# Exp of the routing logits comes third in its list, and early rows' turns and one piece move ahead of the last waits

## The chip, the cores and the metric

The kernel runs on one core of one Trainium2 chip. The metric is the device time of one execution in microseconds (us). The times shown are those of whole executions; the profile is of one further execution, with its own time.

## What is computed

Attention over short windows feeds a mixture of experts with one expert for each token. The arithmetic that matters here, cut from the reference:

```python
# attention: q, k, v are (4, 8, 768, 64); 8 memory rows are in front of each window
for c in range(S // 32):                       # chunks of 32 queries
    k_full = concat(mem_k, k[32*c - 16 : 32*c + 40])
    a = softmax(q_c @ k_full.T / 8)            # sum + 1e-9
    out[c] = a @ v_full
x = out.transpose(0, 2, 1, 3).reshape(3072, 512)
# mixture of experts: 8 experts, 512 -> 1024 -> 512
logits = x @ w_gate
expert_idx = argmax(logits)
probs = exp(logits - max); probs /= probs.sum() + 1e-9
y = relu(x @ w1[expert_idx]) @ w2[expert_idx]
return probs[expert_idx] * y
```

## The kernel before

**Attention.** The 3,072 tokens are 32 blocks of 96 queries. One loop runs over the blocks; its order was written out by hand (`tc.manual_schedule()`), so each engine does its work in the order in which the code issues it. In step `i`, TensorE (PE) makes the scores of block `i`, turns (transposes) the queries of block `i + 2` (`turn_q`), multiplies the first four heads of block `i - 1` by the values (`values(i - 1, 0)`), turns the result `x` of block `i - 2` (`turn_xb`), makes the gate logits of block `i - 3`, does the other four heads (`values(i - 1, 1)`), and turns the keys of block `i + 4` (`turn_k`). ScalarE (ACT) makes the exponentials of the scores (L676, tile `ex`), copies turned queries out of PSUM (L627, `qT`) and turned `x` (L699, `xT`). VectorE (DVE) divides by the softmax sums (L690 and L692, into `xr`), copies turned keys (L645, `kT`) and logits (L1065, `lg`).

**Routing.** The blocks form seven groups (6, 6, 5, 5, 4, 3, 3 blocks). When a group's last logits are there, `routed(g)` puts a list of small steps into `work`: kind "v" for DVE, "p" for PE, "s" for a scatter. `routing(n, kinds)` takes up to `n` steps from the front while their kind is in `kinds`. The loop calls it three times in each step: for a "p" before the values, for 3 "v" steps (5 after step 23) between `values(i - 1, 0)` and `turn_xb`, and for 5 (6 after step 23) at the end, behind `turn_k`. The "v" steps are `top` (L727), `eq` (L731), `weigh` (L734), `first` (L738), `one` (L741, which also issues GpSimd's (POOL) running counts `seen`, L743) and `less` (L746, a subtraction on DVE followed by the Exp of the logits on ACT, L747); then come `total`, `guard`, `inverse` and the labels (L767 to L779). The "p" step `rank` multiplies `onehot` and `seen` on PE; `own`, `row` and `where` (L756 to L763) make row numbers of it. `hold_back` moves "s" steps from the front of `work` to `spread`, and `scatter_some(1)` issues one of these on POOL's queue: an indirect DMA that writes a block's rows of `xr` to `x_dram` (L801), issued only behind PE's latest instruction in program order.

**Early rows.** After 22 blocks, up to 256 rows of expert 0 are gathered from `x_dram` by two indirect DMAs (L880, tile `xe0`). When they are there, PE works on them to fill its waits: `early_ops` holds two turns (`turn_early`, tile `tx`, copied by ACT at L993 into `x0T`), eight pieces of the first layer (`first(f)`, tile `ph`, eight matmuls of 128x256 each, ended by ACT's Relu at L1005), and eight of the second layer (tile `py`, L1014). `do_early(n)` issues the next `n`.

**The tail.** After the loop, the last blocks are finished by hand-ordered lines (from `room_for_x()` on): values and logits of the last blocks, routing of the last two groups, counts of all experts (`count_up`), five gathers of expert 0's rows (`fetch_x(0)`), with early pieces in between. Then eight experts run one after the other, each as products on PE that are planned beforehand. The turned tiles of the attention phase (`tqk`, `tx`) share two PSUM buffers (`ps_t`) in rotation; logits, values and ranks share two banks (`ps_o`); early pieces use the two buffers of the scores (`ps_s`).

Between these lines stand SyncE's (SP) loads: queries, keys and values for the blocks, weights of expert 0 from step 24 on (two pieces of 512 KB in a step), and two loads of 2 MB for expert 1 at the start of the tail.

Of the kernel before, what the change touches and what calls it, by code (L numbers as in the profile page):

```python
# [504 lines left out]
def ordinary(ctx, tc, q, k, v, mem_k, mem_v, moe_w_gate, moe_w1, moe_w2, out, good):  # L505
# [187 lines left out]
    def turn_xb(i):  # L693
        s = st[i]
        tx = ps_t.tile([128, DM // 128, QB], F32, tag="t", name="tx")
        for c in range(DM // 128):
            turn(tx[:, c], s["x"][:, 128 * c : 128 * c + 128], ident[0:QB, 0:QB])
        s["xT"] = apool.tile([128, DM // 128, QB], F32, name="xT")
        nc.scalar.copy(s["xT"], tx)  # L699
# [18 lines left out]
    def routed(g):  # L718

        t0, t1 = GROUPS[g]  # L720
        n, sl = t1 - t0, slice(t0, t1)
        revs = bc(rev[0:QB], 1, n)
        s = {}

        def top():
            s["top"] = small([QB, n], "ltop")
            nc.vector.reduce_max(s["top"], lgs[g], axis=AX_X)  # L727

        def eq():
            s["eq"] = small([QB, n, E], "eq")  # L730
            nc.vector.tensor_tensor(s["eq"], lgs[g], bc(s["top"], 2, E), op=OP.is_equal)  # L731

        def weigh():
            nc.vector.tensor_tensor(s["eq"], s["eq"], revs, op=OP.mult)  # L734

        def first():
            s["first"] = small([QB, n], "first")
            nc.vector.reduce_max(s["first"], s["eq"], axis=AX_X)  # L738

        def one():  # L740
            nc.vector.tensor_tensor(onehot[:, sl], revs, bc(s["first"], 2, E), op=OP.is_equal)  # L741
            for t in range(t0, t1):
                nc.gpsimd.tensor_tensor(seen[:, t + 1], seen[:, t], onehot[:, t], op=OP.add)  # L743

        def less():
            nc.vector.tensor_tensor(lgs[g], lgs[g], bc(s["top"], 2, E), op=OP.subtract)  # L746
            nc.scalar.activation(lgs[g], lgs[g], AF.Exp)  # L747

        def rank():
            rk = s["rk"] = cur["bank"][0:QB, 4 * (D + 1) : 4 * (D + 1) + n * E].rearrange("p (t e) -> p t e", e=E)  # L750
            mm(rk, lhsT=tri[0:QB, 0:QB], rhs=onehot[:, sl], start=True, stop=False)
            mm(rk, lhsT=ones[0:QB, 0:QB], rhs=seen[:, sl], start=False, stop=True)

        def own():
            s["own"] = small([QB, n, E], "own")
            nc.vector.tensor_tensor(s["own"], s["rk"], onehot[:, sl], op=OP.mult)  # L756

        def row():
            s["row"] = small([QB, n], "row")
            nc.vector.reduce_sum(s["row"], s["own"], axis=AX_X)  # L760

        def where():
            nc.vector.tensor_copy(dest[:, sl], s["row"])  # L763

        def total():
            s["total"] = small([QB, n], "total")
            nc.vector.reduce_sum(s["total"], lgs[g], axis=AX_X)  # L767

        def guard():
            nc.vector.tensor_scalar(s["total"], s["total"], 1e-9, None, op0=OP.add)  # L770

        def inverse():
            s["inv"] = small([QB, n], "tinv")
            nc.vector.reciprocal(s["inv"], s["total"])

        def labels(a, e):
            def put():
                nc.vector.tensor_copy(xr[:, a % NXR : a % NXR + e - a, DM + 1], s["inv"][:, a - t0 : e - t0])
                nc.gpsimd.tensor_copy(xr[:, a % NXR : a % NXR + e - a, DM].bitcast(I32), token[0:QB, a:e])  # L779

            return put

        puts = []
        for a in range(t0, t1):
            if a == t0 or a % NXR == 0:
                puts.append(("v", labels(a, min(t1, (a // NXR + 1) * NXR))))
        v = [("v", f) for f in (top, eq, weigh, first, one, less)]
        u = [("v", f) for f in (total, guard, inverse)] + puts
        w = [("p", rank)] + [("v", f) for f in (own, row, where)]
        return v + u + w + [("s", lambda t=t: scatter_one(t)) for t in range(t0, t1)]  # L790
# [38 lines left out]
    def routing(n, kinds="v"):  # L829
        while work and n and work[0][0] in kinds:  # L830
            kind, f = work.pop(0)
            f()
            n -= kind != "s"

    def hold_back():

        while work and work[0][0] == "s":
            spread.append(work.pop(0)[1])

    def scatter_some(n):  # L840
        while spread and n:
            spread.pop(0)()
            n -= 1
# [180 lines left out]
    def do_early(n):  # L1024
        for _ in range(min(n, len(early_ops))):
            early_ops.pop(0)()

    with tc.manual_schedule():
        load_k(0)
        load_q(0)  # L1030
        load_v(0)
        load_k(1)
        load_v(1)
        load_q(1)
        load_k(2)
        load_v(2)
        load_q(2)
        turn_k(0)
        turn_k(1)
        turn_q(0)  # L1040
        turn_q(1)
        for i in range(NB):
            if i % 2 == 0 and i // 2 + 3 < NSB:
                load_q(i // 2 + 3)
            if i % 2 == 1 and (i + 7) // 2 - 1 < NSB and (i + 7) // 2 - 1 >= 3:
                load_k((i + 7) // 2 - 1)
            need(i + 3, load_v)
            scores(i)
            scatter_some(1)
            if i == 0:  # L1050
                turn_k(2)
                turn_k(3)
            need(i + 2, turn_q)
            banks = [ps_o.tile([128, 512], F32, tag="o", name="o") for _ in range(2)]
            cur["bank"] = banks[0]
            routing(1, "p")
            if i >= 1:
                values(i - 1, 0, banks[0])
            routing(5 if i > 23 else 3)
            need(i - 2, turn_xb)  # L1060
            late = logits(i - 3, banks[1]) if i >= 3 else None
            if i >= 1:
                values(i - 1, 1, banks[1])
            if late:
                nc.vector.tensor_copy(*late)  # L1065
            scatter_some(1)
            need(i + 4, turn_k)
            routing(6 if i > 23 else 5)
            hold_back()
            for g in range(len(GROUPS)):  # L1070
                if i - 3 == GROUPS[g][1] - 1:
                    work.extend(routed(g))
            if i == 24:
                fetch_w(0, 4)
            if i >= 24:
                fetch_piece(1)
                fetch_piece(1)
            if len(scatters) >= EARLY and "early" not in cur:
                cur["early"] = i
                early_count(banks[0])  # L1080
                early_gather()

        early_rows()
        n = NB

        def bank_pair():
            banks = [ps_o.tile([128, 512], F32, tag="o", name="o") for _ in range(2)]
            cur["bank"] = banks[0]
            return banks

        room_for_x()
        banks = bank_pair()
        values(n - 1, 0, banks[0])
        routing(1, "p")
        scatter_some(1)
        turn_xb(n - 2)
        late = logits(n - 3, banks[1])
        values(n - 1, 1, banks[1])  # L1100
        scatter_some(1)
        nc.vector.tensor_copy(*late)
        routing(99, "v")
        fetch_w(1, 1)
        fetch_piece(99)
        turn_xb(n - 1)
        banks = bank_pair()
        late = logits(n - 2, banks[1])
        nc.vector.tensor_copy(*late)
        hold_back()  # L1110
        do_early(2)
        scatter_some(1)
        routing(1, "p")
        routing(99, "v")
        hold_back()
        banks = bank_pair()
        late = logits(n - 1, banks[1])
        nc.vector.tensor_copy(*late)
        work.extend(routed(len(GROUPS) - 1))
        routing(99)  # L1120
        check_sums()
        do_early(2)
        scatter_some(1)
        routing(1, "p")
        routing(99, "v")
        hold_back()
        do_early(1)
        scatter_some(1)
        count_up()
        fetch_x(0)  # L1130
        first_sums()
        while spread:
            do_early(1)
            scatter_some(1)
        index = [nc.tensor.value_load(cases[0:1, e : e + 1], min_val=0, max_val=len(ARMS) - 1) for e in range(E)]
        rv = nc.values_load(good[0:1, 0:1], min_val=0, max_val=1)
        tc.switch_hint({mybir.EngineType.PE: index[0]}, len(ARMS), "expert0")
        nc.tensor.addr_align(PAGE, 0, 0)
        do_early(len(early_ops))
# [470 lines left out]
```

## Time and profile before

| | |
|---|---|
| Time of the kernel before, 3 runs | median 545.87 us (544.91 to 546.52) |
| Profiled execution, its own time | 544.41 us |
| Its span, first to last instruction | 542.4 us |
| Outside the span | 2.0 us |
| PE busy | 509.0 us, 94% of the span |
| DVE, ACT, POOL busy | 301.1, 244.7 and 155.5 us (56%, 45%, 29%) |
| Attention loop, from the first scores | 12.5 to about 157 us |
| Tail up to expert 0's first turn | about 157 to 200.4 us |
| Experts | 200.4 us to the end |
| Mean granted clock of TensorE | 0.988 |

Times in the profile count from the first instruction. "PEld" is the load of a matmul's stationary operand, which overlaps PE. In a timeline, a line reads: start, length, engine, line of the kernel, operation, tile written, tiles read, shapes, count; a bracket gives the idle time of the engine before it and what ended it. "L511" and "L516" are the two helpers through which all matmuls and turns go, so PE's lines are told apart by their tiles.

### The profile page before, as it was taken

The page shows a single profiled execution, that of the slowest core. Times are in us where ns is not written, and L with a number is a line of the kernel's source. Part 1 is how long each engine was busy: PE and PEld are TensorE (multiplying, and loading weights), DVE is VectorE, ACT ScalarE, POOL GpSimd, SP SyncE. Part 2 cuts the span into 40 slices and gives each one's busy share as a digit, 9 for nine tenths or more (in the row PEclk, how much of TensorE's full clock was granted, in tenths as well). Part 3 has the DMA queues.
Part 4 walks back from the last instruction along what each step waited for, and adds up shares of the span by engine and source line. Part 5 has one row for each costly group of instructions (what it writes and reads, how often), then busy time and mean ns, then how long its engine had stood idle before and what let it go on. Part 6 is the DMA issues. An engine that isn't in the chain of part 4 may idle for free.

```text
span 542.4 us, 9575 instructions
## 1 busy us (share of the span) xinstructions
PE 509.0 (94%) x3666; PEld 475.4 (88%) x3666; DVE 301.1 (56%) x567; ACT 244.7 (45%) x443; POOL 155.5 (29%) x186
## 2 busy tenths in 40 slices
PE   3889999999989989999999999999999999999991
PEld 2789999999988649999999999987779999999980
DVE  3445666566544517868846457543634777853610
ACT  2446565655632126466553264244215637454311
POOL 2000031313354513526134134212322434412002
PEclk9999999999997999999999999999999999999997
DMA  9999998999992310554615154340415344300002
GB/s 158 173 176 177 156 210 173 206 177 294 283 364 102 95 26 39 188 180 171 219 38 190 39 187 167 109 177 30 181 27 195 118 132 186 79 15 12 1 1 82
DMA packets 81348, 75.01 MB, mean 138 GB/s; under 512 B 39542, under 2 KB 64374, under 8 KB 81280
## 3 DMA queue, kind: packets, MB, share of 16 engines
q1 hardware_dynamic: 71840, 54.60, 41.0%
q0 software_dynamic: 8768, 19.29, 10.8%
q8 instruction: 46, 0.75, 0.6%
q10 hardware_dynamic: 672, 0.18, 0.1%
q14 instruction: 22, 0.18, 0.1%
HBM read 66.13 MB, written 17.50 MB: 154 GB/s over the span
## 4 chain that ended last, share of the span: by engine, by line
PE 81%; issue 9%; DMA 4%; POOL 2%; ACT 1%; DVE 1%; SPq 1%; POOLq 0%; another core or an unknown queue 0%
PE sum_p L511 20%; PE sum_r L511 13%; PE sum_q L511 13%; PE o L511 11%; PE sc L511 7%; PE tqk L516 4%; PE sum_x L516 3%; PE ph L511 3%; DMA kn<-in_k_dram 3%; PE py L511 3%; PE sum_q L516 2%; PE tx L516 2%; POOL out_dram L1275 2%; DMA cst<-c_pack 1%; ACT qT L627 1%
## 5 line engine op out<-in xcount | busy, mean ns | idle before, releaser
L1275 POOL DMA_INDIRECT out_dram<-y,xe x42 | 50.9, 1211 | 181.6 <-PE sum_q L511 62.6
L1292 POOL DMA_INDIRECT xe<-x_dram,rows x35 | 50.6, 1446 | 49.9 <-PE sum_r L511 29.3
L676 ACT ACTIVATE ex<-sc,cst 128x256 f32<-128x256 f32 x96 | 38.4, 470 | 49.9 <-PE sc L511 48.5
L1226 ACT COPY sum_r<-sum_p 128x640 f32<-128x640 f32 x48 | 32.5, 677 | 47.4 <-PE sum_p L511 45.6
L511 PE MATMUL o<-v,ex 128*96 128x65 f32 x512 | 53.9, 249 | 0.0
L511 PE MATMUL sc<-qT,kT 128*128 128x192 f32 x256 | 49.3, 337 | 1.5 <-ACT qT L627 1.5
L511 PEld LDWEIGHTS o<-v,ex 128*96 128x96 f32 x512 | 48.5, 165 | 0.0
L511 PE MATMUL sum_p<-xsT,w 128*128 128x136 f32 (+6 forms) x256 | 47.6, 329 | 0.5
L801 POOL DMA_INDIRECT x_dram<-xr,dest x32 | 30.1, 942 | 59.0 <-PE tqk L516 29.8
L511 PE MATMUL sum_r<-t,w 128*128 128x136 f32 (+6 forms) x256 | 45.8, 326 | 0.0
L511 PE MATMUL sum_p<-t,s 128*128 128x136 f32 (+6 forms) x256 | 45.6, 326 | 0.0
L511 PE MATMUL sum_q<-t,s 128*128 128x136 f32 (+6 forms) x256 | 45.1, 324 | 0.0
L645 DVE COPY kT<-tqk 64x384 f32<-64x384 f32 x64 | 35.5, 554 | 15.6 <-PE tqk L516 14.9
L511 PEld LDWEIGHTS sum_p<-xsT,w 128*128 128x128 f32 x256 | 39.7, 190 | 4.8 <-issue 2.1
L511 PE MATMUL sum_p<-h,w 128*128 128x136 f32 (+6 forms) x256 | 43.8, 324 | 0.0
L511 PEld LDWEIGHTS sc<-qT,kT 128*128 128x128 f32 x256 | 42.0, 195 | 1.9 <-issue 1.4
L511 PEld LDWEIGHTS sum_p<-t,s 128*128 128x128 f32 x256 | 39.7, 190 | 2.6
L511 PEld LDWEIGHTS sum_r<-t,w 128*128 128x128 f32 x256 | 39.6, 190 | 2.6
L511 PEld LDWEIGHTS sum_q<-t,s 128*128 128x128 f32 x256 | 39.8, 190 | 2.3
L511 PEld LDWEIGHTS sum_p<-h,w 128*128 128x128 f32 x256 | 39.5, 190 | 2.3
L1223 DVE TENSOR_TENSOR h<-sum_p,kept 128x640 f32<-128x640 f32 x16 | 13.2, 824 | 48.4 <-ACT sum_r L1226 45.9
L690 DVE RECIPROCAL inv_all<-o 96x4 f32<-96x4 f32 x64 | 11.4, 179 | 48.2 <-PE o L511 43.1
(151 smaller groups left out, 919.3 us busy)
## 6 DMA issues: line engine op xcount, KB each, us to landing
w<-in_moe_w_dram SPq DMA_DIRECT2D x14, 2048.0 KB
kn<-in_k_dram SPq DMA_DIRECT2D x16, 384.0 KB
qn<-in_q_dram SPq DMA_DIRECT2D x16, 384.0 KB
w<-in_moe_w_dram SPq DMA_DIRECT2D x8, 512.0 KB
v<-in_v_dram SPq DMA_DIRECT2D x24, 128.0 KB
v<-in_v_dram SPq DMA_DIRECT2D x24, 112.0 KB
v<-in_v_dram SPq DMA_DIRECT2D x8, 144.0 KB
v<-in_v_dram SPq DMA_DIRECT2D x8, 96.0 KB
```

Source lines behind the costliest of these rows:

```text
L511: i = nc.tensor.matmul(*args, **more)
L516: i = nc.tensor.transpose(*args)
L627: nc.scalar.copy(to[:, :, :, t], tq[D * t : D * t + D])
L645: i = nc.vector.tensor_copy(to, of[:, :, 0:PAIRS].rearrange("d a (y z p) -> d a y z p", y=2, z=2))
L676: nc.scalar.activation(ex4[:, :, :, sl], sc4[:, :, :, sl], AF.Exp, bias=mask[:, 3 * x + g : 3 * x + g + 1], scale=D**-0.5)
L690: nc.vector.reciprocal(inv, o[:, :, D])
L801: i = nc.gpsimd.indirect_dma_start(out=x_dram, out_offset=bass.IndirectOffsetOnAxis(ap=dest[:, t : t + 1], axis=0), in_=xr[:, t % NXR].bit ...
L1223: op(eng, one_op(lambda: engines[eng].tensor_tensor(out, a, b, op=how)), reads, writes)
L1226: op("ACT", one_op(lambda: nc.scalar.copy(to, of)), reads, writes)
L1275: return nc.gpsimd.indirect_dma_start(out=out, out_offset=bass.IndirectOffsetOnAxis(ap=which.bitcast(I32), axis=0), in_=y, in_offset=None, ...
L1292: return nc.gpsimd.indirect_dma_start(out=x[:, g].bitcast(I32), out_offset=None, in_=x_dram, in_offset=bass.IndirectOffsetOnAxis(ap=rows[: ...
```

## The change

In `routed`, `less` (subtraction and Exp) moves from sixth to third place, ahead of `weigh`, `first` and `one`. In the tail, one call of `routing(1, "p")` and one of `hold_back()` are taken out; the two early turns, which were issued together, are issued one before the logits of block 30 and one after them; the turn of block 31 (`turn_xb(n - 1)`) moves from ahead of these logits to behind both early turns; and the first early piece moves ahead of the rank of group 5 and of the logits of block 31.

```diff
@@ in routed
-        v = [("v", f) for f in (top, eq, weigh, first, one, less)]
+        v = [("v", f) for f in (top, eq, less, weigh, first, one)]
@@ in the tail
         room_for_x()
         banks = bank_pair()
         values(n - 1, 0, banks[0])
-        routing(1, "p")
         scatter_some(1)
         turn_xb(n - 2)
         late = logits(n - 3, banks[1])
...
         routing(99, "v")
         fetch_w(1, 1)
         fetch_piece(99)
-        turn_xb(n - 1)
+        do_early(1)
         banks = bank_pair()
         late = logits(n - 2, banks[1])
         nc.vector.tensor_copy(*late)
-        hold_back()
-        do_early(2)
+        do_early(1)
+        turn_xb(n - 1)
         scatter_some(1)
+        do_early(1)
         routing(1, "p")
         routing(99, "v")
         hold_back()
         banks = bank_pair()
         late = logits(n - 1, banks[1])
         nc.vector.tensor_copy(*late)
         work.extend(routed(len(GROUPS) - 1))
```

## The prediction

> **What bounds the kernel now.** I read the page first: PE is busy 94% of the span and is 81% of the chain that ended last, so the time changes where PE idles or runs slowly. Then I asked who PE waits for in the attention loop, 30 to 158 us (columns: who waited, for whom, us in total, times, longest):
>
> ```profile
> PE tqk L516 <- ACT qT L627: 1.6, 3, 0.7
> ```
>
> This is the only wait, three times. To see where, I cut the loop into its steps, from one block's scores to the next (columns: stretch, length, then busy us of PE, PEld, DVE, ACT, POOL, granted clock, DMA share, GB/s), with one stretch of the tail:
>
> ```profile
> 55.35:59.67 4.32, 4.32 (x46) 4.30 (x45) 2.81 (x11) 2.67 (x6) 0.00 (x0) 1.00 1.02 202
> 59.67:64.65 4.98, 4.53 (x46) 4.38 (x45) 4.09 (x17) 2.61 (x8) 1.31 (x7) 1.00 1.24 176
> 64.65:69.31 4.66, 4.66 (x51) 4.64 (x49) 2.32 (x8) 2.73 (x7) 0.00 (x0) 1.00 0.71 132
> ...
> 86.62:91.61 4.99, 4.54 (x47) 4.38 (x45) 4.11 (x17) 2.63 (x8) 1.31 (x7) 1.00 1.26 193
> ...
> 109.25:114.51 5.26, 4.54 (x47) 4.39 (x45) 4.25 (x19) 2.73 (x7) 2.07 (x7) 1.00 0.99 259
> ...
> 163.78:170.61 6.83, 6.08 (x24) 5.33 (x25) 3.56 (x21) 1.39 (x4) 2.65 (x10) 0.50 0.34 119
> ```
>
> A plain step takes 4.32 us and a step with a rank 4.66. Three steps take 4.98, 4.99 and 5.26. They are the steps in which groups 0, 1 and 2 reach their Exp. The timeline of the second shows how:
>
> ```profile
> 85.83 0.20 DVE L734 TENSOR_TENSOR eq<-eq,cst 96x48 f32<-96x48 f32 x1
> ...
> 86.16 0.48 ACT L699 COPY xT<-tx 128x384 f32<-128x384 f32 x1
> ...
> 88.72 0.20 DVE L746 TENSOR_TENSOR lg<-lg,ltop 96x48 f32<-96x48 f32 x1
> ...
> 88.95 0.24 ACT L747 ACTIVATE lg<-lg 96x48 f32<-96x48 f32 x1 [2.32 <-DVE lg L746]
> 89.10 1.18 ACT L676 ACTIVATE ex<-sc,cst 128x256 f32<-128x256 f32 x3
> ...
> 90.17 0.99 ACT L627 COPY qT<-tqk 64x384 f32<-64x384 f32 x2
> ...
> 91.22 0.55 PE L516 MATMUL tqk<-cst,kn 96*128 96x96 f32 x4 [0.45 <-ACT qT L627]
> ```
>
> `less` is sixth, so it falls behind `turn_k`'s copies on DVE and starts at 88.72. ACT idles 2.32 us in front of the Exp although the next scores are already there; `ex`, the copies `qT` and the PSUM buffer that they free are all late, and PE stands still for 0.45 us.
>
> In the tail, PE's timeline:
>
> ```profile
> 159.96 0.39 PE L516 MATMUL tx<-cst,xr 96*128 96x96 f32 x2 [0.32 <-issue]
> 162.21 0.39 PE L516 MATMUL tx<-cst,xr 96*128 96x96 f32 x2 [1.87 <-DVE xr L692]
> 162.43 0.77 PE L511 MATMUL o<-wg,xT 128*96 128x8 f32 x8
> 163.06 0.63 PE L516 MATMUL tx<-cst,xe 128*128 128x128 f32 x4
> 163.93 1.11 PE L516 MATMUL tx<-cst,xe 128*128 128x128 f32 x4 [0.24 <-issue]
> 164.84 0.41 PE L511 MATMUL o<-onehot,cst 96*96 96x24 f32 x2
> 165.84 0.51 PE L511 MATMUL o<-seen,ones 96*96 96x24 f32 x2 [0.60 <-issue]
> 166.18 1.43 PE L511 MATMUL o<-wg,xT 128*96 128x8 f32 x8
> 167.46 5.25 PE L511 MATMUL ph<-x0T,w 128*128 128x256 f32 x16
> ```
>
> Turn of block 31 in two halves, logits of 30, early turns, rank in two halves with a wait for POOL's `seen` between, logits of 31, first pieces. Idle here: 0.32 + 1.87 + 0.24 + 0.60 = 3.03 us. From 163.78 to 170.61 the clock is at half (the last windows line): 6.08 us of PE work there cost 6.08 / 2 = 3.04 us. Nothing later hides this, as the chain shows PE pieces without a break until the experts begin:
>
> ```profile
> 175.15 8.74 PE ph L511 x40
> 183.89 6.87 PE py L511 x16
> ```
>
> Expert 0's rows are no bound: their last gather is issued at 191.63 and its landing stands in the trace's semaphore records at 194.8, while PE first reads them at 200.38.
>
> [...] I read the first early gather, issued at 155.75, as landed at 161.97 (semaphore records), with the weights' traffic at a DMA share over 1.
>
> **Part 1, `less` third.** DVE's third step of group 1 ran at 85.83 to 86.03. ACT's `qT` copies before it end at 86.13, so the Exp (0.24 us) starts without a wait and pushes `xT` from 86.16 to about 86.4. Its readers are the logits at 89.27, and its buffer is wanted again at 87.95: hidden by 1.3 us; without that cover it costs 0.24 us a group. `weigh`, `first`, `one` move 0.2 us later; `seen` ended at 90.46 and the rank came at 93.27: hidden. The three long steps fall to 4.325: (4.98 - 4.325) + (4.99 - 4.325) + (5.26 - 4.325) = **2.25 us**. Groups 3 and 4 have no such stall (group 3's step takes 4.67, the rank alone): 0. DVE's `total` no longer waits 0.3 us; in the tail DVE then waits 1.9 us for the rank anyway: 0. No DMA's order changes here.
>
> **Part 2, calls without effect.** The `routing(1, "p")` taken out finds a "v" in front, the `hold_back()` a "p", and `scatter_some(1)` an empty list: 0 from both sides, since nothing is issued. SP's order is the same. POOL's scatters keep their order; each stays behind a PE piece, now one piece further in the list.
>
> **Part 3, the order on PE.** Placed on before's clock. The first early turn waits for its gather: 162.03 (bounds: after 159.64, when PE becomes free, and before 163.06, where it ran without waiting; I take the semaphore records). 0.44 us, then logits of 30 to 163.10. The second early turn waits for its gather, 163.24 by the same records: 163.29 to 163.75. The turn of 31 (its `xr` was ready at 162.16, the buffer is free after ACT's `x0T`, about 163.5) to 164.1, or 164.4 at half clock. Piece 0 follows when the second `x0T` is there, about 164.35. It covers the `seen` wait (ready at 166.07). Then rank, logits of 31, pieces 1 and 2. Idle: 2.39 + 0.19 + up to 0.3 against 3.03[...]. With the clock low for the same 6.83 us, summing the durations gives 197.9 for the end of the last early piece, against 198.71: 0.8 less.
>
> The clock is the rest. Between 159.64 and the first dense piece lay 7.8 us[...]; after the change it is 4.7 us[...]. One low window: 197.9 - 1.6 = 196.3; none: 194.8. Gains 0.8, 2.4, 3.9. Cost from below: a third window, 1.7 us of loss. I take **2.0**, one low window or a little better, reduced because before may have had shorter low states in its other runs.
>
> What is queued behind the new waits: behind the early turn, all PE work; behind the Exp on ACT, `xT` alone. The count of experts comes up to 0.8 us later at low clock, with 5.6 us of room before PE reads the gathered rows.
>
> **Sum.** 2.25 + 2.0 = 4.25 us. The profiled execution, 544.41 (span 542.4, 2.0 outside), becomes 540.2. The three runs' median is 1.46 above it; I carry that over: 545.87 - 4.25 = 541.6.
>
> **Rivals.** (A) The transfers don't follow. DMA is saturated from step 24, so the early gathers land at the same absolute time though PE comes 2.25 us earlier, and PE waits in front of the first early turn: the gain is the tail's alone, 0.8 to 2.4: 543.5 to 545.1. For: DMA share over 1 up to 163. Against: share 0.48 in 119 to 123, just before the weights start, so the start of saturation moves along. (B) The Exp stalls in its new place: if DVE is late by a scatter's landing (one such wait of 1.2 us at 104.45), ACT holds `xT` and half the loop's gain goes: 542.8 with the tail. Against: 0.1 us of slack in each group, then 1.3 us in the buffer. (C) Slower: expert 0's rows become the bound. Piece 0 and both turns stand ahead of the last routing; if count, scatters and five gathers slip by more than 5.6 + 4.25 us, PE waits at 200.38. Two more us of slip (11.9) would give 547.9. Against: the order alone shifts the count by under 1 us.
>
> **Numbers.** 0.3% is 1.64 us, about what a measurement can tell. Forecast 0.72, A 0.14, B 0.10, C 0.04. Forecast and B lie over 1.64 below; of A about half. Faster 0.87, same 0.08, slower 0.05. Range: from both parts at their best (2.25 + 3.9 = 6.2: 539.7) to A's upper part, 544.2.
>
> **What would show it.** Steps of groups 0 to 2 at 4.33, no PE wait for `qT`, Exp about 86 in this clock; piece 0 ahead of the rank; no idle of 0.60 in the rank; a low clock of one window or none. Wrong if the long steps stay, if PE's wait at the first early turn grows past 2.4 us, or if the low clock lasts as long or longer.

## The result, and the profile after

| | before | after |
|---|---|---|
| Time, median of 17 runs each | 545.56 us (543.50 to 547.52) | 542.33 us (540.92 to 545.72) |
| Profiled execution, and its span | 544.41 / 542.4 us | 542.90 / 540.8 us |
| Loop, scores of block 3 to scores of block 31 | 123.94 us | 123.25 us |
| Tail, scores of block 31 to expert 0's first turn | 47.03 us | 45.03 us |
| From there to the end | 342.06 us | 342.17 us |

The ratio is 0.9949, interval 0.9935 to 0.9963: about 2.8 us less (the medians lie 3.23 apart). The forecast was 4.25 less. Two slow executions of over 1,300 us, one of the kernel before and one of the list alone, are in no ratio. In the two profiles, 0.69 comes from the loop and 2.00 from the tail; 0.96 is lost before block 3, where the change has nothing (over the kernels of this study that start moved between 29.4 and 30.5 us).

Whom PE waited for, 30 to 194 us, of the kernel after (who, for whom, us in total, times, longest):

```profile
PE tx L516 <- DVE xr L692: 1.2, 1, 1.2
PE o L511 <- POOL seen L743: 0.7, 1, 0.7
PE tx L516 <- DMA xe<-x_dram,rows: 0.6, 1, 0.6
PE tqk L516 <- DMA kn<-in_k_dram: 0.5, 1, 0.5
```

The wait for `qT`, three times in the kernel before, is gone. The wait for `seen` is in the loop, and it is new there. The one for `kn` is at 30 us, ahead of block 3. The loop cut into steps shows both (columns as before: stretch, length, busy us of PE, PEld, DVE, ACT, POOL, clock, DMA share, GB/s):

```profile
56.32:60.65 4.33, 4.33 (x48) 4.31 (x45) 2.82 (x11) 2.65 (x7) 0.00 (x0) 1.00 1.16 174
60.65:64.97 4.32, 4.32 (x47) 4.30 (x45) 3.54 (x15) 2.82 (x7) 1.34 (x7) 1.00 1.23 167
86.93:91.26 4.33, 4.33 (x48) 4.31 (x45) 3.55 (x15) 2.84 (x7) 1.31 (x7) 1.00 1.24 195
108.90:113.23 4.33, 4.33 (x47) 4.31 (x45) 3.73 (x17) 2.83 (x7) 2.03 (x7) 1.00 0.94 252
130.85:136.83 5.98, 5.09 (x50) 4.77 (x49) 3.67 (x16) 2.80 (x7) 1.12 (x6) 1.00 1.12 299
149.34:153.62 4.28, 4.24 (x43) 4.13 (x42) 2.82 (x16) 2.08 (x5) 1.67 (x9) 1.00 1.04 355
161.95:168.78 6.83, 6.80 (x27) 5.97 (x28) 1.71 (x12) 1.87 (x4) 3.17 (x7) 0.50 0.43 149
```

Lines two to four are the steps that took 4.98, 4.99 and 5.26 us: they now cost what a plain step costs (line one). Lines five and six are the steps with the ranks of groups 3 and 4, which took 4.67 and 4.05 us before: 1.31 and 0.23 us were lost there. The last line is the low clock of the tail: 0.50 for 6.83 us, as long as before (163.78 to 170.61, also at 0.50).

The timeline of group 1's step, of the kernel after:

```profile
86.14 0.20 DVE L746 TENSOR_TENSOR lg<-lg,ltop 96x48 f32<-96x48 f32 x1
...
86.46 0.24 ACT L747 ACTIVATE lg<-lg 96x48 f32<-96x48 f32 x1
...
86.73 0.48 ACT L699 COPY xT<-tx 128x384 f32<-128x384 f32 x1
...
88.52 1.20 ACT L676 ACTIVATE ex<-sc,cst 128x256 f32<-128x256 f32 x3 [1.32 <-PE sc L511]
...
89.61 1.01 ACT L627 COPY qT<-tqk 64x384 f32<-64x384 f32 x2
...
90.92 0.50 PE L516 MATMUL tqk<-cst,kn 96*128 96x96 f32 x4
```

The Exp of the logits starts right behind the copies of `qT` on ACT, `xT` follows it, `ex` waits for its scores alone, and PE's turn of `kn` carries no bracket.

Group 3's step, where the new loss is. First the stretch of the kernel before (columns as above), then the timeline of the kernel after:

```profile
132.12:136.79 4.67, 4.67 (x52) 4.65 (x49) 3.77 (x16) 2.66 (x8) 1.05 (x6) 1.00 1.11 320
```

```profile
132.57 0.20 DVE L741 TENSOR_TENSOR onehot<-cst,first 96x40 f32<-96x40 f32 x1
...
132.82 0.36 PE L511 MATMUL o<-onehot,cst 96*96 96x40 f32 x2
...
132.85 1.29 POOL L743 TENSOR_TENSOR seen<-seen,onehot 96x8 f32<-96x8 f32 x5 [3.64 <-DVE onehot L741]
...
133.93 0.36 PE L511 MATMUL o<-seen,ones 96*96 96x40 f32 x2 [0.74 <-POOL seen L743]
```

For i over 23 a step gives five calls in its first half. They used to be `top`, `eq`, `weigh`, `first`, `one`; with `less` third, `one` is the sixth and falls behind `turn_k`'s copies `kT` on DVE. `onehot` is ready at 132.57, POOL needs 1.29 us for `seen`, and the rank, PE's next work, stands waiting for it. Of the 1.31 us lost, 0.74 is this wait, 0.15 idle time ahead of the rank's first half, and 0.42 longer busy time (5.09 us against 4.67).

PE's timeline in the tail of the kernel after:

```profile
159.55 0.38 PE L516 MATMUL tx<-cst,xr 96*128 96x96 f32 x2 [1.24 <-DVE xr L692]
159.77 0.77 PE L511 MATMUL o<-wg,xT 128*96 128x8 f32 x8
160.39 0.87 PE L511 MATMUL o<-v,ex 128*96 128x65 f32 x8
161.89 1.10 PE L516 MATMUL tx<-cst,xe 128*128 128x128 f32 x4 [0.62 <-DMA xe<-x_dram,rows]
162.78 1.34 PE L511 MATMUL o<-wg,xT 128*96 128x8 f32 x8
163.97 1.09 PE L516 MATMUL tx<-cst,xe 128*128 128x128 f32 x4
164.86 0.85 PE L516 MATMUL tx<-cst,xr 96*128 96x96 f32 x4
165.74 3.48 PE L511 MATMUL ph<-x0T,w 128*128 128x256 f32 x8
169.05 0.27 PE L511 MATMUL o<-onehot,cst 96*96 96x24 f32 x2
169.17 0.33 PE L511 MATMUL o<-seen,ones 96*96 96x24 f32 x2
```

Two waits are left, 1.24 for block 30's `xr`, which the kernel before does not have, and 0.62 for the early rows. From 161.89 on PE has work without a break, at a clock of 0.50 from 161.95 to 168.78 (piece 0 takes 3.48 us; at a clock of 1.00 it takes 1.99, in the run with the loads held). The rank's second half follows its first at once: its `seen` is covered by piece 0.

### The profile page after: what moved, and what is told of

Same layout as the page of the kernel before. It is cut to its first block, busy times and chain, and to the rows that moved or that the text cites. A ratio compares the mean times of both kernels' runs of the same rounds, so it can differ in the third digit from the quotient of the medians.

```text
span 540.8 us, 9574 instructions
## 1 busy us (share of the span) xinstructions
PE 511.9 (95%) x3666; PEld 478.7 (89%) x3666; DVE 300.6 (56%) x567; ACT 245.4 (45%) x443; POOL 155.7 (29%) x186
## 4 chain that ended last, share of the span: by engine, by line
PE 81%; issue 9%; DMA 5%; POOL 2%; DVE 1%; SPq 1%; ACT 0%; POOLq 0%
PE sum_p L511 20%; PE sum_r L511 13%; PE sum_q L511 13%; PE o L511 11%; PE sc L511 7%; PE tqk L516 3%; PE sum_x L516 3%; DMA kn<-in_k_dram 3%; PE ph L511 3%; PE py L511 3%; PE sum_q L516 2%; PE tx L516 2%; POOL out_dram L1275 2%; DMA xe<-x_dram,rows 1%; DMA cst<-c_pack 1%
## 5 line engine op out<-in xcount | busy, mean ns | idle before, releaser
L511 PE MATMUL sc<-qT,kT 128*128 128x192 f32 x256 | 50.6, 343 | 1.2 <-ACT qT L627 1.2
L511 PEld LDWEIGHTS sc<-qT,kT 128*128 128x128 f32 x256 | 43.2, 199 | 1.4 <-issue 1.4
```

The costliest lines, as they stand in the source:

```text
L511: i = nc.tensor.matmul(*args, **more)
```

## The experiments

All ratios are against the kernel before, run on the same chip, from 6 to 22 executions of each kernel. Four questions: what each half of the change is worth; whether the late `one` explains the missing gain; what the low clock in the tail hangs on; what the early piece ahead of the rank does.

**The list alone** (the kernel before, with only the list changed):

```diff
-        v = [("v", f) for f in (top, eq, weigh, first, one, less)]
+        v = [("v", f) for f in (top, eq, less, weigh, first, one)]
```

> The list's new order alone, the tail as before. Theory 1 (both parts count, and the list takes back most of what it gives): steps 10, 16 and 21 fall to 4.33 (2.25 us gained), step 26 stays long at about 6.0 because group 3's `one` has left the first half of its step (1.3 us lost) and step 30 loses 0.2: 0.7 us gained in the loop, ratio about 0.9985. Rival (the list carries the whole gain, the tail's order is noise of the clock): 3 us gained, ratio 0.9945.

Measured: 545.35 us, ratio 0.9993 (0.9978 to 1.0008). Its profile has the three steps at 4.32, 4.32 and 4.33 us, and step 30 at 4.27. Step 26 took 6.97 because in this execution a low clock began at 135.42, 1.80 us after the end of the same wait of 0.74 us for `seen`, and lasted 6.83 us. So in the steps the list by itself gains its 2.25 us and gives 1.54 of it back. By the ratio, what is left is between 1.2 us less and 0.4 us more. A lower clock may be a part of that: its mean granted clock was 0.9804 over 13 executions, against 0.9821 for the kernel before.

**The tail alone** (the kernel after, with the old list):

```diff
-        v = [("v", f) for f in (top, eq, less, weigh, first, one)]
+        v = [("v", f) for f in (top, eq, weigh, first, one, less)]
```

> The tail's new order alone, the list as before. Theory 1: 2.0 us gained, all of it between the last scores and expert 0's first turn (47.0 us before, 45.0 after); ratio about 0.9963; the three long steps stay at 4.98, 4.99 and 5.26 and step 26 is back at 4.67. Rival (the list carries it all): no gain, ratio 1.000.

Measured: 543.07 us, ratio 0.9956 (0.9939 to 0.9973), about 2.4 us. The two halves add: 0.0007 + 0.0044 = 0.0051, the whole change's own figure. Each of the two is known to within 0.0017 only, so a small overlap between them is not excluded.

**One kept early** (the kernel after; the first half gives one call more for i over 23):

```diff
-            routing(5 if i > 23 else 3)
+            routing(6 if i > 23 else 3)
...
-            routing(6 if i > 23 else 5)
+            routing(5)
```

> The changed kernel with the two halves of late steps swapped, 6 routing steps first and 5 at the end, so that `one` stays in the first half of the step for groups 3 and 4. Theory 1: step 26 goes from 5.98 back to about 4.67 and step 30 from 4.28 to about 4.05, 1.3 to 1.5 us less than the changed kernel: ratio about 0.992. Rival (step 26 was held by something else, such as the clock or the loads of that time): step 26 stays near 6.0 and the ratio stays at 0.995.

Measured: 541.21 us, ratio 0.9923 (0.9898 to 0.9947). Steps 26 and 30 are back at 4.66 and 4.05. Its timeline of step 26:

```profile
131.70 0.20 DVE L741 TENSOR_TENSOR onehot<-cst,first 96x40 f32<-96x40 f32 x1
...
131.98 1.31 POOL L743 TENSOR_TENSOR seen<-seen,onehot 96x8 f32<-96x8 f32 x5 [1.67 <-DVE onehot L741]
...
133.60 0.29 PE L511 MATMUL o<-onehot,cst 96*96 96x40 f32 x2
...
133.71 0.34 PE L511 MATMUL o<-seen,ones 96*96 96x40 f32 x2
```

`onehot` comes at 131.70, ahead of `kT`; `seen` ends at 133.29 and PE asks for it at 133.71. The interval overlaps that of the whole change a little, so the same edit was also made where the tail is old.

**The list, with one kept early, on the old tail** (the list edit and the edit above, nothing else):

> The kernel before with less third in the list and with the first half of a step giving six calls instead of five for i over 23, so that one of groups 3 and 4 keeps its place; the tail is the old one. Theory: the list alone was worth 2.25 us in steps 10, 16 and 21 and lost 1.54 us in steps 26 and 30; with one kept early the 2.25 us are left whole: 543.4 us, ratio 0.996, against 0.9993 for the list alone. Rival, that the three steps' gain is given back further on even so (a later clock window, a transfer in the tail): ratio 0.998 to 1.000.

Measured: 543.07 us, ratio 0.9948 (0.9929 to 0.9968), against 0.9993 for the list alone. The intervals don't meet. Here the list does what was forecast for it: 1.7 to 3.9 us less.

**The loads held.** In the tail of the kernel after, SP issues expert 1's two loads of 2 MB ahead of the early turns. Here they stand behind them:

```diff
-        fetch_w(1, 1)
-        fetch_piece(99)
         do_early(1)
         banks = bank_pair()
...
         do_early(1)
+        fetch_w(1, 1)
+        while pieces:
+            behind(pieces.pop(0)())
         turn_xb(n - 1)
```

> The changed kernel with the two 2 MB loads for expert 1 held until PE has done the second early turn. Theory 1 (in the tail PE waits for the early rows[...]): the gathers land within about 3 us of their issue instead of 6.5, PE waits under 0.5 us before the early turns, and the tail falls from 45.0 to about 43: ratio about 0.991. If the late notices of PE's products (1.0 to 2.2 us late between 157 and 161 us in both kernels) come from the same traffic, they go too. Rival (the tail is bound by PE's own work at half clock, or by POOL's queue): the tail stays at 45 and the ratio at 0.995.

Measured: 538.86 us, ratio 0.9877 (0.9858 to 0.9896). PE's timeline in its tail:

```profile
159.15 0.74 PE L516 MATMUL tx<-cst,xr 96*128 96x96 f32 x4
...
161.07 0.60 PE L516 MATMUL tx<-cst,xe 128*128 128x128 f32 x4
161.51 0.77 PE L511 MATMUL o<-wg,xT 128*96 128x8 f32 x8
162.13 0.63 PE L516 MATMUL tx<-cst,xe 128*128 128x128 f32 x4
163.27 0.55 PE L516 MATMUL tx<-cst,xr 96*128 96x96 f32 x4 [0.50 <-ACT x0T L993]
163.75 1.99 PE L511 MATMUL ph<-x0T,w 128*128 128x256 f32 x8
```

Its last scores start at 154.80. The early gathers landed 3.15 and 4.52 us after them (semaphore records), against 8.23 and 9.19 in the kernel after; the DMA share over 153 to 165 us is 0.33 against 0.95. PE waits 0.50 us in all, and the clock is 1.00 in every stretch from 153 to 180 us. The experts pay nothing for the later weights: 342.30 us against 342.17.

The late notices of which the expectation speaks shrink too. DVE's division of the attention's values waits for PE's semaphore. For the last three halves (the second of block 30, both of block 31) it began up to 2.20 us after PE's products had ended in the trace of the kernel after, up to 1.89 in the kernel before, and 0.19 at most here. These lags make the waits for `xr`: 1.40 us for block 30 ahead of the 1.24 us wait after, 1.89 for block 31 ahead of the 1.87 us wait before. In the four profiles with the loads held the longest lag is 0.04 to 0.34 us, in seven of the other eight 0.66 to 2.20; but in the list with one kept it is 0.04 too. So the loads are a likely cause, not a shown one.

**Both mends together** (one kept early, loads held):

> The changed kernel with both mends at once: one stays early for groups 3 and 4 (steps 26 and 30 at 4.66 and 4.05 us), and expert 1's two 2 MB loads wait for the second early turn. If the two losses are independent, as the two runs alone suggest (1.5 us in steps 26 and 30; 4.6 us in the tail), the times add: about 1.4 us below the run with the held loads alone, 537.4 us, ratio 0.985, tail 40.4 us, clock never low in it. If they are one loss seen twice (a rank that comes earlier only meets a clock or a transfer that is later), the ratio stays at 0.988.

Measured: 537.74 us, ratio 0.985 (0.9823 to 0.9877), the best of the study: 8.2 us under the kernel before, 5.4 us (0.985 against 0.9949) under the kernel after. Steps 26 and 30 at 4.66 and 4.05, tail 40.25, no low clock in it. The mends add: 0.0026 and 0.0072 alone, 0.0099 together.

**The loads held in the kernel before** (old list, old order in the tail):

> The kernel before (list and tail order unchanged), with only expert 1's two 2 MB loads held until after the second early turn. Theory of the gathers: they land some 3 to 5 us after the last scores instead of 8 to 9, TensorE doesn't wait in the tail and the low clock goes, so the old order gains most of it too: tail 42 to 43 us, 541.0 us, ratio 0.991; steps 10, 16 and 21 stay at 4.98, 4.99 and 5.26. Rival, that the new order is what makes the early gathers useful: in the old one the turns stand behind the rank, tail 45 us or more, ratio 0.996 to 1.000.

Measured: 544.90 us, ratio 0.9981 (0.9967 to 0.9995). The theory fell and the rival held: the tail is 45.93. The gathers did land early, 3.36 and 4.54 us after the last scores, but in the old order PE reaches the first early turn only at 8.16 us: it stands behind the turn of block 31, and waits for `xr` (0.56 us), `seen` (0.74) and the later 0.81 us stay. The clock was low for 6.83 us all the same. Here the early gathers were worth little, a tail 1.10 us shorter against 4.64 in the new order, since the old order has PE reach the early turns late.

**PE kept busy** (the kernel after, with 16 products of 128x256 that nothing reads, where PE waits):

```diff
+        def keep_warm(k):
+            to = ps_s.tile([128, 2, 512], F32, tag="s", name="warm")[:, 0, 0:NER]
+            for j in range(k):
+                mm(to, lhsT=ident, rhs=cst[:, 0:NER], start=j == 0, stop=j == k - 1)
...
+        keep_warm(6)
         scatter_some(1)
...
+        keep_warm(6)
         do_early(1)
         banks = bank_pair()
...
+        keep_warm(4)
         do_early(1)
         turn_xb(n - 1)
```

> The changed kernel with 16 matmuls of 128x256 from constants whose result nothing reads, put where TensorE would wait in the tail: 6 after the last values, 6 ahead of the first early turn, 4 ahead of the second. Theory of the clock: the low clock in the tail follows from the little work of TensorE there; with fillers it is shorter or gone, which is worth 3.4 us, and the fillers cost 1 to 1.5 us where the wait doesn't cover them: 540.3 us, ratio 0.991. Rival, the gathers alone set it and the clock does not follow the fillers: they only cost their time, 543.3 us, ratio 0.997.

Measured: 544.89 us, ratio 0.9986 (0.9972 to 1.0000). PE's timeline of it:

```profile
158.50 2.81 PE L511 MATMUL warm<-cst 128*128 128x256 f32 x12
161.14 0.49 PE L516 MATMUL tx<-cst,xr 96*128 96x96 f32 x4
...
162.81 2.81 PE L511 MATMUL warm<-cst 128*128 128x256 f32 x12
...
166.51 1.97 PE L511 MATMUL warm<-cst 128*128 128x256 f32 x8
```

The clock does not fall in this tail, with the loads where they were and the gathers as late as before (8.12 and 9.14 us after the last scores): from 157.50 to 160.91 PE was busy 3.41 of 3.41 us, at a clock of 1.00 and a DMA share of 1.05. In the kernel after, PE was busy 1.78 of the 3.41 us up to the fall at 161.95, at the same DMA share of 1.05. Over all executions the mean granted clock is 0.9909 here (22) and 0.9845 in the kernel after (17). With the loads held in the kernel before it is 0.9829 (22), against 0.9822 (59) without. So in these runs the clock went with PE's own work, not with the transfers. The net loss is a size that I had wrong: a product is two matmuls in the trace, 32 in all, and from start to next start they took 2.64 + 2.64 + 1.81 = 7.09 us. They took away 3.41 us of low-clock loss (half of 6.83) and 1.52 of waits and cost 7.09.

**Without the early piece ahead of the rank** (the kernel after, one line less):

```diff
         do_early(1)
         turn_xb(n - 1)
         scatter_some(1)
-        do_early(1)
         routing(1, "p")
```

> The changed kernel without the early piece that stands ahead of the rank (the two early turns stay ahead of it). Theory: the wait of the rank for the last ones mask (0.6 us) and the wait of 0.8 us among the early pieces for the index loads both come back, the tail is 1 to 1.4 us longer, 543.5 us, ratio 0.997. Rival, the piece only changes places with the rank and what it costs in one place it saves in the other: 542.4 us, ratio 0.995.

Measured: 545.21 us, ratio 0.9991 (0.9975 to 1.0008): nearly all that the change gained is gone, more than expected. The tail is 2.64 us longer. The timeline of this kernel:

```profile
192.24 0.69 ACT L1014 ACTIVATE y<-py,xe 128x512 f32<-128x512 f32 x1 [6.53 <-PE py L511]
...
192.98 0.70 PE L511 MATMUL py<-w,h 128*128 128x512 f32 x1 [0.83 <-issue]
```

The 0.83 us between the two halves of `py` are back, and the low clock lasted 10.24 us, not 6.83: another 1.7 us. Together these are 2.5 of the 2.64 us. The rank's wait did not return in this profile. The 0.8 us wait stands in the profile of all six kernels here without a piece ahead of the rank, and in none of the six with it. PE resumes 0.05 us after ACT's first `y` ends; the profile names no releaser. My expectation called it a wait for index loads, which nothing here shows.

**Without the piece, loads held:**

> The run with expert 1's loads held behind the second early turn, without the early piece ahead of the rank. Theory: the piece is worth the wait for the index loads among the later pieces (0.8 us) and the rank's wait for its mask (0.5 us); what the run without the piece lost beyond that was one more window of low clock (1.7 us)[...]: tail 41.5 us, ratio 0.990, and the clock stays full in the tail. Rival, the piece's own place is worth over 2 us whatever the loads do: tail 42.5 us or more, ratio 0.992 or more.

Measured: 543.33 us, ratio 0.9944 (0.9922 to 0.9965), against 0.9877 with the piece: 3.7 us. The rival held. PE's timeline:

```profile
162.07 0.27 PE L511 MATMUL o<-onehot,cst 96*96 96x24 f32 x2
163.61 0.35 PE L511 MATMUL o<-seen,ones 96*96 96x24 f32 x2 [1.27 <-POOL seen L743]
163.80 0.82 PE L511 MATMUL o<-wg,xT 128*96 128x8 f32 x8
164.48 5.39 PE L511 MATMUL ph<-x0T,w 128*128 128x256 f32 x16
...
188.71 7.13 PE L511 MATMUL py<-w,h 128*128 128x512 f32 x16 [0.80 <-issue]
```

With everything earlier, the rank meets POOL's `seen` 1.27 us too soon; the clock is low for 3.41 us from 165.32, so two pieces take 5.39 us (with both mends, at a clock of 1.00, 3.70), and 0.80 us come back later: 1.27 + 1.71 + 0.80 = 3.8 us. The tail is 3.88 us longer.

**The tails side by side.** For each profile: the tail, PE's waits in it (those over 0.1 us, without the 1.7 us for the last `y` that all have), the length of low clock, and what remains of the tail after the waits, half the low clock and that last wait are taken off.

| kernel | ratio | tail | waits | low clock | remains |
|---|---|---|---|---|---|
| before | 1 | 47.03 | 3.83 | 6.83 | 38.10 |
| after | 0.9949 | 45.03 | 1.86 | 6.83 | 38.06 |
| list alone | 0.9993 | 46.24 | 1.73 | 10.24 | 37.69 |
| tail alone | 0.9956 | 45.75 | 1.18 | 10.24 | 37.66 |
| one kept early | 0.9923 | 43.64 | 2.07 | 3.41 | 38.17 |
| loads held | 0.9877 | 40.39 | 0.50 | 0 | 38.19 |
| both mends | 0.9850 | 40.25 | 0.50 | 0 | 38.05 |
| before, loads held | 0.9981 | 45.93 | 2.53 | 6.83 | 38.30 |
| kept busy | 0.9986 | 46.95 | 0.34 | 0 | 37.81 (7.09 of products off too) |
| no piece | 0.9991 | 47.67 | 2.69 | 10.24 | 38.06 |
| list, one kept | 0.9948 | 48.02 | 3.46 | 10.24 | 37.76 |
| held, no piece | 0.9944 | 44.27 | 2.57 | 3.41 | 38.21 |

The remainder is the same within 0.65 us in all twelve. So the tail is 38 us of PE work, plus its waits, plus half its low clock, and little else. Each row is one execution, and the low clock varies between executions; the ratios are of many.

## Why the prediction was right, and where not

**Direction and range: right.** 542.33 lies between 539.7 and 544.2. The gain was two thirds of the forecast, 2.8 against 4.25 us.

**"The three long steps fall to 4.325": right.** 2.25 us, by the mechanism named: the Exp starts at 86.46, forecast "about 86", no wait for `qT` is left, and rival B (the Exp stalls in its new place) has nothing for it in the trace.

**"`weigh`, `first`, `one` move 0.2 us later; `seen` ended at 90.46 and the rank came at 93.27: hidden" and "Groups 3 and 4: 0": this is the step that failed.** The cover was read from group 1, where a step gives three calls first and five later. For groups 3 and 4 the first half gives five, so the moved `less` did not push `one` by 0.2 us but out of the half, behind `kT` on DVE. `onehot` ended 1.92 us after the step's first scores (132.77 against 130.85); where `one` keeps its place it ends 0.04 us ahead of them (131.90 against 131.94). The 1.29 us of `seen` then came between it and the rank. Loss 1.31 + 0.23 = 1.54 us in the profile. Keeping `one` in its half moved the ratio from 0.9993 to 0.9948 on the old tail and from 0.9949 to 0.9923 on the new one. On the new tail the kernel with `one` kept gains 4.2 us by its ratio (2.9 to 5.6), about what the whole change was forecast to give. That 4.25 - 1.54 = 2.7 lies so close to the measured 2.8 is in part luck, since the tail's term came out by other parts than forecast.

**The tail, "I take 2.0": the sum came out, its terms did not.** The profiles have 2.00 us, but with the low clock at the same 6.83 us, for which the prediction had 0.8. That it lasts as long was one of the prediction's own signs of being wrong. In this pair the clock gives none of the 1.2 us that it was taken for, and the waits give all: they fell from 3.83 to 1.86. That the sum is 2.0 all the same is luck. The prediction's "one low window" is 3.41 us of low clock, half of the 6.83 seen before; that the new order would come down to it was the author's estimate.

As to the low clock: the stretch from the last values to piece 0 was forecast at 4.7 us and came out at 4.48 (161.26 to 165.74). But PE had waited before these values too, 1.24 us up to 159.55 for block 30's `xr`, which no term of the prediction had. No trace shows how short such a stretch has to be for the clock to stay at 1.00.

The pair is not typical, though. The profiled execution of the kernel before had a granted clock of 0.988, as high as any of 59 executions of it, whose mean is 0.9822; the mean of the kernel after is 0.9845. The difference, 0.0023 of 541 us, is 1.2 us. This is an estimate of the most that the clock gave on average, and it counts the kernel's start and end too. How the tail's gain divides between waits and clock is therefore open.

The wait of 0.80 between the halves of `py` was left out of the 3.03 us of before, where the pieces were read as being without a break (the chain of the kernel before has 0.80 us of "issue" at 190.75, right behind the two lines shown); it goes with the early piece ahead of the rank, as six kernels against six show. And the waits after the change are 1.86 in all, where the prediction had up to 2.9. Piece 0 ahead of the rank goes with less low clock: without it the low clock was 3.41 us longer in both pairs of profiles (10.24 against 6.83, and 3.41 against none with the loads held), and the mean granted clock lower (0.9809 against 0.9845, and 0.9871 against 0.9892).

**Rival A (the transfers don't follow) fell in its size.** PE's wait at the first early turn is 0.62 us, under the 2.4 named as the limit. This pair of profiles tests the rest poorly: the gather landed at 161.84 against 161.97, but the last scores came no earlier (153.62 against 153.35). In the list with one kept they came 1.29 us earlier than before (152.06), and the gather landed 1.56 earlier (160.41): there the transfers followed. What the rival pointed at is still the larger prize: with the 4 MB of weights behind the gathers the new order gains 3.9 us more, and in both profiles that have this order with the early piece the tail has no low clock.

**Rival C (expert 0's rows) fell.** Expert 0's first turn waits 1.7 us for ACT's last `y`, as before.

**Open.** In the tail of the kernel after, block 30's second half turn waits 1.24 us for `xr`, in other runs between none and 0.6. In the trace DVE idles 2.40 us ahead of that block's division, until 158.86, 1.40 us after PE's products had ended; what delays the notice was not tried by itself. Nor was it tried why PE resumes with `y` in the six kernels without the piece.

## What to carry to other kernels

When a call moves up in a list that is handed out in portions, look at which call falls out of each portion, for every portion size in use, and at what stands between the portions on that engine: a cover read from one group says nothing of a group with another split. In the tail of this kernel a saved wait was worth more than its length when the low clock went with it: with the loads held PE waited 0.50 us instead of 1.86, the 6.83 us of low clock were gone, and the tail was 4.64 us shorter. Dense work that is ready can stand ahead of a wait: the one early piece ahead of the rank made the tail 2.64 us shorter, and 3.88 with the loads held. A transfer that small gathers had to follow could wait until they had landed (ratio 0.9877 against 0.9949 in the new order), but that paid little where the work that uses them was not queued early too (0.9981 in the old order).

## What was not expected of the hardware

Where the tails had a low clock, it lasted 3.41, 6.83 or 10.24 us, which is one, two or three times 3.41. In the kernel before and in the kernel after it was 0.50 for 6.83 us. In the kernel before, the two falls at 163.78 and 535.84 lie 372.06 us apart, 109 times half of the 6.83 us (6.827 in the clock record); in the kernel after the falls at 161.95 and 534.01 lie as far apart.

Ahead of the late fall at 535.84 PE was idle for all of 3.41 us. In the tail it was not: of the 3.41 us ahead of the fall it was busy 1.48 in the kernel before, 1.78 in the kernel after, 2.14 in the one with the loads held and no piece, 2.80 in the tail alone, and in one loop step 2.52 (the list alone; five other profiles have the same step with the same wait and no low clock, the kernel after with the same 2.52 us at 1.00). The longest single wait in the tail, the last `y` aside, was 1.87 us in the kernel before and 1.24 in the kernel after.

PE's busy time alone does not decide it. In the run with both mends PE was busy 6.32 us of the 6.82 from 156.50 on, in the second half 2.91 of 3.41, and the clock stayed at 1.00. The wait of 1.7 us for the last `y`, between the products `py` and the turns of expert 0, did not lower it in the pair: it was 1.00 from 196 to 203 us in the kernel before and from 186 to 205 us in the kernel after. So the low clock came behind waits of 0.74 us (the list alone, in the loop) to 1.87 us (the kernel before) among turns and small products, and not in every execution; what else decides is not shown.
